# Expert 0's first layer with joint products for both parts of x, its results weighed by ScalarE, and the list work moved among the late tiles

## The chip, the cores and the metric

The kernel runs on one core of a Trainium2 chip. The metric is the device time of the whole program in microseconds (us). Engines are named as the profile names them: PE is TensorE's matmuls, PEld its weight loads, DVE is VectorE, ACT ScalarE, POOL GpSimd, SP SyncE, which issues DMAs. Each engine works through its own queue in the order in which the program was written.

## What is computed

Retention attention over 4 sequences of 768 tokens and 8 heads, whose rows are the tokens of a mixture of experts with one expert for each token:

```python
state = gamma * state + einsum(k_t, v_t);  y_t = scale * (q_t @ state)    # 3072 rows of 512
logits = x @ w_gate;  expert = argmax(logits);  gate_w = softmax(logits)[expert]
for e in range(8):
    h = maximum(x[mask] @ w1[e], 0)          # 512 -> 1024
    out[mask] = gate_w[mask] * (h @ w2[e])   # 1024 -> 512
```

Every float32 product of the experts is made of three: a number is cut into a high and a low part (`whi`, `wlo`; `xh`, `xl`; `hh`, `hl`), and TensorE adds up `whi*xh + wlo*xh + whi*xl` in one PSUM tile.

## The kernel before

The program runs in one pass that is written out by hand: what stands earlier in the code stands earlier in the queue of its engine, and nothing else sets the order.

**Retention** (`retention_moe`, up to 95 us of the profile) goes through 24 chunks of 128 tokens in 12 pairs k = 0 to 11. As tokens are finished, their expert is chosen in groups (`gating`), and GpSimd scatters their rows into a list of each expert in DRAM (`send_x`).

**Expert 0 is worked in two halves**, so that TensorE has work while the last lists are made. The **early half** (`early_half`) takes the first 192 tokens (EARLY) of expert 0. `hidden(f, part)` makes one of the 8 feature tiles of 128 with 12 matmuls of 192 columns (L823), each behind a weight load of its own; ScalarE then takes Relu into `rx` (L827) and a cast into `hh` (L828), and `low` subtracts to make `hl` (L831), for four tiles on VectorE and for four on GpSimd. `fill(n)` puts halves of tiles between the steps of the last gating. `result` is the second layer of 128 tokens, 24 matmuls of 512 columns (L841), weighed on VectorE (L845). The **late half** is e = 0 of `moe_main`: 224 tokens (LATE), 64 (BESIDE) of which share a row tile with the early rest. Its first layer is 8 tiles of 12 matmuls of 224 columns (L1052) into three PSUM tiles `phs` in turn; Relu and low part are made in two pieces of 64 and 160 columns (L1064, L1066). Its second layer has two row tiles of 24 matmuls (L1105), weighed on VectorE (L960), and a third one if the list is long.

**Lists.** Which experts come in which order (`eid`), where their lists end (`end`), how many tokens each has (`limit`) and by how much of its widest shape it stays short (`spare`) is worked out by some 16 small VectorE operations (L669 to L728) in the early half. TensorE's queue reads two of these numbers with loads of its own (`count_columns`, L896 and L897), called in late tile 4, and then branches over the four widths of expert 1's matmuls (`by_count`).

**Late x.** The late list is read from DRAM into `xg1`; VectorE transposes it in two pieces (L782), ScalarE casts one piece (L791) and VectorE the other (L718) to the high part, VectorE subtracts for the low part (L792, L720).

**Weights** come in parts of 1024 rows' worth, each cut by `split`: a ScalarE cast to `whi` (L172) and a VectorE subtraction to `wlo` (L174). Numbers 8 to 15 of expert 0's splits are halves of its second layer; of expert 1's parts, 0 is cut in late tiles 3 and 4, 1 in late tile 7, 2 beside the late second layer. `prep_x` transposes and cuts expert 1's x behind late tile 7. `jobs[f]` holds what is written behind late tile f (0 to 7) or behind step f - 8 of the second layer.

## Time and profile before

| | us |
|---|---|
| time, median of 3 runs | 386.64 (385.94 to 388.25) |
| the profiled execution, whole | 384.25 |
| its span in the profile | 382.40 |
| PE busy | 376.3 (98%) |
| DVE busy | 260.2 (68%) |
| the last 64 matmuls of the early first layer | 101.11 to 108.25 |
| early second layer | 108.25 to 113.77 |
| late first layer | 113.77 to 124.55 |
| late second layer | 124.55 to 135.66 |
| expert 1's first layer begins | 135.66 |

Times within the profile are from the start of its span. A row of the timeline gives start, length, engine, line, operation, output <- inputs, shape, and after an x how many instructions stand in it. Successive rows of PE overlap: the spacing of two starts, not a row's length, tells what a matmul costs TensorE.

### The profile page before, as it was taken

How to read it: one execution, taken by the hardware profiler on the slowest of the kernel's cores; microseconds unless marked ns; L12 is line 12 of the kernel's file. 1: busy time of each engine (PE TensorE's matmuls, PEld its weight loads, DVE VectorE, ACT ScalarE, POOL GpSimd, SP SyncE). 2: the span in 40 equal slices, each digit the busy share in tenths (PEclk: the TensorE clock that was granted, in tenths of full speed). 3: DMA queues.
4: the chain of work that ended last, by engine and by line, in shares of the span. 5: the costliest groups of instructions: out<-in, count | busy, mean ns of one | idle time of the engine just before them, and what ended most of it. 6: DMA issues, size and time to landing. Idle time of an engine off the chain costs nothing. (4 is left out here: it accounts for less than half of the span.)

```text
span 382.4 us, 8977 instructions
## 1 busy us (share of the span) xinstructions
PE 376.3 (98%) x3276; PEld 354.0 (93%) x3276; DVE 260.2 (68%) x571; ACT 154.8 (40%) x315; POOL 167.7 (44%) x149
## 2 busy tenths in 40 slices
PE   8999999999999999999999999999999999999994
PEld 5888888888989899999999999999999999999984
DVE  4548868798898786666675667486757767776511
ACT  3345445454734454334433542353434335444200
POOL 0332445647721230003853484357528444652754
PEclk9999999999999999999999999999999999999999
DMA  8998999997359765545664656366656756761111
GB/s 287 417 405 345 327 407 358 413 373 267 144 128 220 238 213 156 194 162 150 170 197 137 175 166 219 100 188 181 192 159 170 221 176 177 192 196 59 51 49 59
DMA packets 35237, 80.67 MB, mean 211 GB/s; under 512 B 5487, under 2 KB 19443, under 8 KB 33112
## 3 DMA queue, kind: packets, MB, share of 16 engines
q1 hardware_dynamic: 29892, 66.87, 54.0%
q0 software_dynamic: 5264, 12.69, 9.1%
q8 instruction: 58, 0.95, 1.1%
q14 instruction: 19, 0.16, 0.1%
q10 hardware_dynamic: 4, 0.01, 0.0%
HBM read 65.07 MB, written 15.19 MB: 210 GB/s over the span
## 5 line engine op out<-in xcount | busy, mean ns | idle before, releaser
L772 POOL DMA_INDIRECT out<-Z,sidx x82 | 104.8, 1278 | 120.5 <-DVE Z L991 102.9
L174 DVE TENSOR_TENSOR wlo<-raw,whi 128x1024 fp32r<-128x1024 f32 (+1 forms) x72 | 78.6, 1100 | 5.3 <-ACT whi L172 4.5
L1064 ACT ACTIVATE hh<-ph 128x64 fp32r<-128x64 f32 (+7 forms) x72 | 32.4, 461 | 91.5 <-PE ph L1052 91.5
L172 ACT CAST whi<-raw 128x1024 fp32r<-128x1024 f32 (+1 forms) x72 | 67.0, 952 | 5.2 <-DMA raw<-w 3.3
L1107 PE MATMUL py<-hh,wlo 128*128 128x392 f32 (+4 forms) x192 | 66.1, 344 | 0.0
L1107 PE MATMUL py<-hl,whi 128*128 128x392 f32 (+4 forms) x192 | 66.0, 344 | 0.0
L1107 PE MATMUL py<-hh,whi 128*128 128x392 f32 (+4 forms) x192 | 66.0, 344 | 0.0
L1066 DVE SCALAR_TENSOR_TENSOR hl<-ph,hh 128x64 fp32r<-128x64 f32 (+7 forms) x72 | 36.4, 515 | 34.1 <-ACT hh L1064 33.6
L1052 PE MATMUL ph<-xh,wlo 128*128 128x392 f32 (+5 forms) x224 | 49.1, 341 | 0.0
L1052 PE MATMUL ph<-xh,whi 128*128 128x392 f32 (+5 forms) x224 | 49.0, 341 | 0.0
L1052 PE MATMUL ph<-xl,whi 128*128 128x392 f32 (+5 forms) x224 | 48.9, 340 | 0.0
L1052 PEld LDWEIGHTS ph<-xh,whi 128*128 128x128 f32 x224 | 40.3, 189 | 0.3
L1052 PEld LDWEIGHTS ph<-xh,wlo 128*128 128x128 f32 x224 | 40.3, 188 | 0.2
L1052 PEld LDWEIGHTS ph<-xl,whi 128*128 128x128 f32 x224 | 40.3, 188 | 0.2
L281 POOL TENSOR_TENSOR vs<-qkv_t,cs 128x512 f32<-128x512 f32 x19 | 20.2, 1063 | 42.7 <-DMA qkv_t<-qkv 32.8
L1107 PEld LDWEIGHTS py<-hh,wlo 128*128 128x128 f32 x192 | 36.1, 188 | 0.2
L1107 PEld LDWEIGHTS py<-hh,whi 128*128 128x128 f32 x192 | 36.1, 188 | 0.2
L1107 PEld LDWEIGHTS py<-hl,whi 128*128 128x128 f32 x192 | 36.1, 188 | 0.2
L791 ACT CAST xh<-xt 128x512 fp32r<-128x512 f32 (+7 forms) x27 | 14.8, 551 | 50.7 <-DVE xt L782 50.7
L295 DVE TENSOR_TENSOR Sb<-sp,xgs 128x512 f32<-128x512 f32 x48 | 30.0, 683 | 4.8 <-PE sp L292 4.7
L772 POOL DMA_INDIRECT xs_dram<-xn,KEY x24 | 25.2, 1050 | 13.3 <-ACT xn L350 4.1
L986 DVE STREAM_TRANSPOSE Z<-py 128x416 f32<-128x416 f32 (+2 forms) x24 | 15.3, 637 | 20.4 <-PE py L1107 20.2
(168 smaller groups left out, 520.6 us busy)
## 6 DMA issues: line engine op xcount, KB each, us to landing
raw<-w SPq DMA_DIRECT2D x64, 512.0 KB
qkv_t<-qkv SPq DMA_DIRECT2D x16, 1024.0 KB
qkv_t<-qkv SPq DMA_DIRECT2D x8, 512.0 KB
qkv_t<-qkv SPq DMA_DIRECT2D x4, 768.0 KB
xgs<-xs_dram SPq DMA_DIRECT2D x12, 211.2 KB
xgs<-xs_dram SPq DMA_DIRECT2D x8, 227.5 KB
out<-Z,sidx POOLq DMA_INDIRECT x82, 3.8
xs_dram<-zero SPq DMA_DIRECT2D x6, 195.0 KB
```

Source lines behind the costliest of these rows:

```text
L172: nc.scalar.copy(out=to[h][:, a:a + n], in_=raw[:, a:a + n])
L174: engine.tensor_tensor(out=to[h][:, a:a + n], in0=raw[:, a:a + n], in1=parts[0][h][:, a:a + n].bitcast(F32), op=ALU.subtract)
L281: engine.tensor_tensor(out=vs, in0=qs[g][:, 2].rearrange("a (h d) -> a h d", d=D), in1=cv[:, c, :].unsqueeze(2).broadcast_to([P, H, D]), o ...
L295: nc.vector.tensor_tensor(out=Sb[:, r], in0=sps[r], in1=M[:, r], op=ALU.mult)
L772: sc = tc.nc.gpsimd.indirect_dma_start(out=out, out_offset=bass.IndirectOffsetOnAxis(ap=index, axis=0), in_=rows, in_offset=None, bounds_c ...
L791: nc.scalar.copy(out=xh[:, :, sl], in_=src)
L986: nc.vector.transpose(out=Zs[e][:, 0:nb, k, :], in_=py[:, 0:32 * nb].rearrange("p (j c) -> p j c", c=32))
L1052: nc.tensor.matmul(out=ph[:, :w], lhsT=sliver(wparts[e, f // 4][a], kd)[:, fo:fo + P], rhs=x[:, kd, :w], start=(n == 0), stop=(n == 3 * KD ...
L1064: nc.scalar.activation(out=to, in_=of, func=AF.Relu)
L1066: nc.vector.scalar_tensor_tensor(out=low, in0=of, scalar=0.0, in1=to.bitcast(F32), op0=ALU.max, op1=ALU.subtract)
L1107: nc.tensor.matmul(out=py[:, :cols], lhsT=sliver(a, f % 4)[:, k * P:(k + 1) * P], rhs=x[:, :cols], **se)
```

## The change

- **Joint products, early.** Tiles 1 to 7 of the early first layer have 4 matmuls `wlo*xh` of 192 columns and 4 matmuls of 384 columns, whose moving side is `xh` and `xl` side by side, with `whi` loaded once; tile 0 stays. The two halves of the PSUM tile are then added: ScalarE copies the second half into `rx`, VectorE adds the first (`join`), ScalarE takes Relu into `hh`, VectorE makes `hl` with max and subtract. All eight lows are on VectorE.
- **Joint products, late.** Tiles 1 to 7 of the late first layer likewise: 4 matmuls of 224 and 4 of 448 columns, a ScalarE copy and a VectorE addition into `sums` (the named `Z`); Relu and low part read `sums`.
- **Results of expert 0** are weighed by ScalarE.
- **Lists.** The 16 small operations leave the early half: they are `chores` of late tiles 0 to 5 (`before`, `numbers`, `ends`, `limits`, `spares`, `places`); `token_index` of the late rows goes from tile 2 to tile 6, the two loads of TensorE's queue from tile 4 to tile 7, part 0 of expert 1's splits behind late tile 7, part 1 into the second layer, part 2 to the second layer's second row tile.
- **Late x** is transposed in two pairs of its four slices, and ScalarE casts both.
- **Sooner.** The last rows are sent before, not behind, the early half's first VectorE work; SP reads the late list before it waits for expert 1's list end; the early list is read before the last parts of expert 0's weights; expert 0's second-layer splits begin one earlier (8 at k = 8).
- **Rank.** The last `rank` has a PSUM tile of another pool; FILL counts matmuls.

```diff
-FILL = (2, 2, 2, 2)
+FILL = (12, 8, 16, 16)
...
-SPLITS = {4: (0, 1), 5: (2, 3), 7: (4, 5), 8: (6, 7), 9: (8, 9), 10: (10,)}
+SPLITS = {4: (0, 1), 5: (2, 3), 7: (4, 5), 8: (6, 7, 8), 9: (9, 10), 10: (11,)}
...
+        products = [(f, i) for f, to in ((0, 8), (1, 4), (0, 12), (1, 8), *((f, 8) for f in range(2, KF)))
+                    for i in range({(0, 12): 8, (1, 8): 4}.get((f, to), 0), to)]
...
+            for f, i in products[state["done"]:state["done"] + n]:
+                hidden(f, i)
+            state["done"] += n
+
+        def joins(n):
+            for f in range(state["joined"], n):
+                join(f)
+            state["joined"] = n
...
             stages[name]()
-        split(0, 2, 3, nc.vector, 1, ("cast",))
         logits(NCH // 2 - 1)
         rows(NCH - 2)
+        finish_logits(NCH // 2 - 1)
         rows(NCH - 1)
-        finish_logits(NCH // 2 - 1)
         for g in range(SENDS[NCH // 2 - 1][1], GROUPS[-1][0]):
             send_x(g)
+        turned_rows = gsm.tile([P, 2], F32, name="turned_rows")
+        at = GROUPS[-1][0] % (2 * CPB)
+        nc.gpsimd.tensor_copy(out=turned_rows, in_=ring[:, at:at + 2, 0, 0])
...
         fill(FILL[1])
-        final["rank"](ps_s, "sp")
+        final["rank"](ps_m, "mm")
         fill(FILL[2])
         final["slots"]()
         final["weights"]()
-        split(0, 2, 3, nc.vector, 1, ("cut",))
-        past = gsm.tile([P, E1], F32, name="past")
+        for g in range(GROUPS[-1][0], NCH):
+            send_x(g)
+        joins(3)
...
         nc.vector.tensor_copy(out=end1, in_=past[:, 0:1])
+        joins(4)
         lows(2, nc.vector)
-        for g in range(GROUPS[-1][0], NCH):
-            send_x(g)
         for i in (12, 13):
-            split(0, *divmod(i, 4), nc.vector, 1)
+            split(0, *divmod(i, 4), nc.vector, 1, ("cast",))
         fill(FILL[3])
-        lows(4, nc.gpsimd)
-        sq = lambda name: gsm.tile([P, E1, E1], F32, name=name)
-        i7 = lambda t: t.unsqueeze(2).broadcast_to([P, E1, E1])
...
+        split(0, 3, 0, nc.vector, 1, ("cut",))
+        joins(5)
+        lows(3, nc.vector)
+        split(0, 3, 1, nc.vector, 1, ("cut",))
+        joins(6)
+        lows(4, nc.vector)
         for i in (14, 15):
-            split(0, *divmod(i, 4), nc.vector, 1)
-
-        nc.vector.tensor_tensor(out=se, in0=sel, in1=s7(past), op=ALU.mult)
-        with nc.allow_low_precision(reason="one nonzero term, an integer below 2**15"):
-            nc.vector.tensor_reduce(out=end7, in_=se, axis=AX.X, op=ALU.add)
+            split(0, *divmod(i, 4), nc.vector, 1, ("cast",))
+        fill(len(products) - state["done"])
...
+        split(0, 3, 2, nc.vector, 1, ("cut",))
+        joins(7)
+        lows(5, nc.vector)
+        split(0, 3, 3, nc.vector, 1, ("cut",))
+        lows(6, nc.vector)
+        joins(KF)
+        lows(KF, nc.vector)
         xg1 = ld.tile([P, NJ8, W], F32, name="xg1", tag="ld")
         xt1 = ld.tile([P, KD, LATE], F32, name="xt1", tag="ld")
         number = lambda i: nc.sync.value_load(eid7[0:1, i - 1:i], min_val=1, max_val=E - 1)
         end_of = lambda t, i: nc.sync.value_load(t[0:1, i - 1:i], min_val=0, max_val=(E9 + 1) * N)
-        past1 = end_of(end1, 1)
         load_x(xg1, E, NJ8)
         load_meta(meta0[EARLY - P:, 1:2], E, 1, 0, BESIDE)
         load_meta(meta0[:, 2:3], E, 1, BESIDE)
         load_meta(meta0[0:32, 3:4], E, 1, BESIDE + P, 32)
         fetch(1, 0)
+        past1 = end_of(end1, 1)
...
+        token_index(sidx0[:, 0:1], meta0[:, 0:1], cnt[:, 0:1])
...
+        xhl1 = new_xhl(LATE)
+        pairs = [slice(k, k + 2) for k in (0, 2)]
+        for ks in pairs:
+            turn_slices(nc, xt1, xg1, 0, LATE, None, ks)
+            nc.scalar.copy(out=xhl1[:, 0, ks], in_=xt1[:, ks])
+        for ks in pairs:
+            nc.vector.tensor_tensor(out=xhl1[:, 1, ks], in0=xt1[:, ks], in1=xhl1[:, 0, ks].bitcast(F32), op=ALU.subtract)
+        result(0, 0)
+        result(0, 1)
+        send(0)
...
+    chores = [before, numbers, ends, limits, spares, places]
...
-    def hidden(f, part):
-        whi, wlo = wparts[0, f // 4]
+    def hidden(f, i):
         fo = (f % 4) * P
-        if part != 1:
-            phs[f] = first if f == 0 else ps.tile([P, EARLY], F32, name="ph0", tag="sp")
-        order = [(a, x, kd) for a, x in ((whi, 0), (wlo, 0), (whi, 1)) for kd in range(KD)]
-        for i, (a, x, kd) in list(enumerate(order))[6 * part:6 * part + 6]:
-            nc.tensor.matmul(out=phs[f], lhsT=sliver(a, kd)[:, fo:fo + P], rhs=xhl[:, x, kd, :],
-                             start=(i == 0), stop=(i == len(order) - 1))
-        if part != 0:
+        whi, wlo = [[sliver(a, kd)[:, fo:fo + P] for kd in range(KD)] for a in wparts[0, f // 4]]
+        if i == 0:
+            phs[f] = first[f] if f < len(first) and first[f] is not None else ps.tile([P, 2 * EARLY], F32, name="ph0", tag="sp")
...
+        if f == 0:
+            todo = alone(whi, 0) + alone(wlo, 0) + alone(whi, 1)
+        else:
+            both = phs[f].rearrange("p (x t) -> p x t", x=2)
+            todo = alone(wlo, 0) + [(both, whi[kd], xhl[:, :, kd, :]) for kd in range(KD)]
+        to, w, x = todo[i]
+        nc.tensor.matmul(out=to, lhsT=w, rhs=x, start=(i == 0), stop=(i == len(todo) - 1), skip_group_check=True)
+        if i == len(todo) - 1:
             h = rx[:, f % 4, :]
-            nc.scalar.activation(out=h, in_=phs[f], func=AF.Relu)
-            nc.scalar.copy(out=hh[f][:, 0:EARLY], in_=h)
+            if f == 0:
+                nc.scalar.activation(out=h, in_=phs[f], func=AF.Relu)
+                nc.scalar.copy(out=hh[f][:, 0:EARLY], in_=h)
+            else:
+                nc.scalar.copy(out=h, in_=phs[f][:, EARLY:2 * EARLY])
+
+    def join(f):
+        h = rx[:, f % 4, :]
+        nc.vector.tensor_tensor(out=h, in0=phs[f][:, 0:EARLY], in1=h, op=ALU.add)
+        nc.scalar.activation(out=hh[f][:, 0:EARLY], in_=h, func=AF.Relu)
 
     def low(f, engine):
-        engine.tensor_tensor(out=hl[f][:, 0:EARLY], in0=rx[:, f % 4, :], in1=hh[f][:, 0:EARLY].bitcast(F32),
-                             op=ALU.subtract)
+        engine.scalar_tensor_tensor(out=hl[f][:, 0:EARLY], in0=rx[:, f % 4, :], scalar=0.0, in1=hh[f][:, 0:EARLY].bitcast(F32),
+                                    op0=ALU.max, op1=ALU.subtract)
...
-        nc.vector.tensor_scalar(out=sliced(yo[:w, j, :]), in0=featured(py[:w]), scalar1=meta0[:w, j, 1:2], scalar2=None,
-                                op0=ALU.mult)
+        nc.scalar.activation(out=sliced(yo[:w, j, :]), in_=featured(py[:w]), func=AF.Copy, scale=meta0[:w, j, 1:2])
...
+        if e == 0:
+            nc.scalar.activation(out=to, in_=turned, func=AF.Copy, scale=share)
+        else:
+            nc.vector.tensor_scalar(out=to, in0=turned, scalar1=share, scalar2=None, op0=ALU.mult)
...
-                job(2, nc.vector.memset, rare[0:widths[0][2]], 0.0)
-                job(2, token_index, sidx0[:, 1:4], meta0[:, 1:4], lim[:, 1:4], "joint")
+                for f, chore in enumerate(chores):
+                    job(f, chore)
+                job(KF - 2, token_index, sidx0[:, 1:4], meta0[:, 1:4], lim[:, 1:4], "joint")
+                job(KF - 1, nc.vector.memset, rare[0:widths[0][2]], 0.0)
                 for i in range(3):
-                    job(1 + i // 2, nc.vector.memset, phs[i][:, CAPS[1] - 3 * STEPS[1]:], 0.0)
+                    job(KF, nc.vector.memset, phs[i][:, 2 * LATE:], 0.0)
                 for j in range(nxt - 1):
                     job(KF - 1, prep_x, 1, j, nc.vector if j % 2 else nc.gpsimd)
...
+                job(4 if e else KF - 1, count_columns, e + 1)
             if e > 0:
...
-                for part, s0 in ((0, 3), (1, KF - 1)):
+                for part, s0, at in ((0, 3, KF - 1), (1, KF - 1, KF)):
                     job(s0, fetch, e + 1, part + 2)
                     for i, eng in halves:
-                        job(s0 + i * (s0 < KF - 1), split, e + 1, part, i, eng)
+                        job(at, split, e + 1, part, i, eng)
...
+                def beside_layer():
...
+                    main = ph[:, 0:LATE]
+                    both = ph[:, 0:2 * LATE].rearrange("p (x t) -> p x t", x=2)
+                    if f == 0:
+                        todo = [(main, a[kd], xh[:, kd]) for kd in range(KD) for a in (whi, wlo)]
+                        todo += [(main, whi[kd], xl[:, kd]) for kd in range(KD)]
+                    else:
+                        todo = [(main, wlo[kd], xh[:, kd]) for kd in range(KD)]
+                        todo += [(both, whi[kd], xhl1[:, :, kd]) for kd in range(KD)]
+                    for i, (to, w, x) in enumerate(todo):
+                        nc.tensor.matmul(out=to, lhsT=w, rhs=x, start=(i == 0), stop=(i == len(todo) - 1),
...
+                if e:
+                    by_count(e, first_layer)
+                else:
+                    beside_layer()
+                    if f == 0:
+                        sums = yp.tile([P, CMAX32 // 32, KD, 32], F32, name="Z").rearrange("p j k r -> p (j k r)")
+                    else:
+                        total = sums[:, f * LATE:(f + 1) * LATE]
+                        nc.scalar.copy(out=total, in_=ph[:, LATE:2 * LATE])
+                        nc.vector.tensor_tensor(out=total, in0=ph[:, 0:LATE], in1=total, op=ALU.add)
...
-                if more and e == 0 and k < 2:
-                    split(e + 1, 2, *halves[k])
+                if more and e == 0 and k == 1:
+                    for h in halves:
+                        split(e + 1, 2, *h)
```

What follows is VectorE's queue, in the program's order, at three places. `hl`, `hh`, `rx`, `xhl` are the parts named above; numbers behind a name tell one buffer from another; `Z` is `sums`; x2 stands for two alike.

**VectorE, from the last weight cuts of expert 0 (L174) to the late list's transposes, before:**

```order
L174 TENSOR_TENSOR wlo<-raw,whi 128x512 x2
L682 TENSOR_TENSOR se<-sel,past 128x49
L684 TENSOR_REDUCE end_84<-se 128x7
L831 TENSOR_TENSOR hl_1669<-rx_1664,hh_1667 128x192 x2
L704 TENSOR_SCALAR third<-cnt 128x1
L705 TENSOR_TENSOR se<-sel,cnt 128x49
L706 TENSOR_REDUCE limit<-se 128x7
L707 TENSOR_TENSOR limit<-limit,cs 128x7
L709 TENSOR_TENSOR fits<-limit,cs 128x21
L712 TENSOR_REDUCE spare<-fits 128x7
L782 STREAM_TRANSPOSE xt_1877<-xg_1876 128x4x4x32
L782 STREAM_TRANSPOSE xt_1877<-xg_1876 128x3x4x32
```

**The same place, after** (L872 is the addition of `join`, L876 the low part):

```order
L872 TENSOR_TENSOR rx_1666<-ph_1877,rx_1666 128x192
L876 SCALAR_TENSOR_TENSOR hl_1671<-rx_1666,hh_1669 128x192
L174 TENSOR_TENSOR wlo<-raw,whi 128x512
L876 SCALAR_TENSOR_TENSOR hl_1671<-rx_1666,hh_1669 128x192
L872 TENSOR_TENSOR rx_1666<-ph_1887,rx_1666 128x192
L876 SCALAR_TENSOR_TENSOR hl_1671<-rx_1666,hh_1669 128x192 x2
L230 TENSOR_SCALAR far<-cs,cnt 128x1
L232 TENSOR_SCALAR ids<-meta_81 128x1
L234 SCALAR_TENSOR_TENSOR sidx_82<-ids,far 128x1
L707 COPY lim<-cnt 64x1
L708 COPY lim<-cnt 64x1
L815 STREAM_TRANSPOSE xt_1909<-xg_1908 128x7x2x32 x2
```

The small list operations between the cuts and the transposes are gone; seven additions and four more low parts stand in the early half, each of which waits for a ScalarE operation, and the row numbers of the early tokens (L230 to L709) now stand ahead of the transposes.

**VectorE, between late tiles 2 and 5, before:**

```order
L1066 SCALAR_TENSOR_TENSOR hl_1668<-ph_2167,hh_1666 128x64
L1066 SCALAR_TENSOR_TENSOR hl<-ph_2167,hh 128x160
L1072 MEMSET between 32x512
L227 TENSOR_TENSOR far<-cs,lim 128x3
L228 TENSOR_SCALAR far<-far 128x3
L232 TENSOR_SCALAR ids<-meta_81 128x3
L1066 SCALAR_TENSOR_TENSOR hl_1668<-ph_2165,hh_1666 128x64
L1066 SCALAR_TENSOR_TENSOR hl<-ph_2165,hh 128x160
L174 TENSOR_TENSOR wlo<-raw,whi 128x1024
L1066 SCALAR_TENSOR_TENSOR hl_1669<-ph_2166,hh_1667 128x64
```

**Late tiles 3 to 5, after** (L1129 is the addition, L1139 the low part):

```order
L743 TENSOR_REDUCE end_84<-se 128x7
L1129 TENSOR_TENSOR Z<-ph_2020,Z 128x224
L1139 SCALAR_TENSOR_TENSOR hl_1670<-Z,hh_1668 128x64
L1139 SCALAR_TENSOR_TENSOR hl<-Z,hh 128x160
L749 TENSOR_SCALAR third<-cnt 128x1
L750 TENSOR_TENSOR se<-sel,cnt 128x49
L751 TENSOR_REDUCE limit<-se 128x7
L752 TENSOR_TENSOR limit<-limit,cs 128x7
L1129 TENSOR_TENSOR Z<-ph_2021,Z 128x224
L755 TENSOR_TENSOR fits<-limit,cs 128x21
L758 TENSOR_REDUCE spare<-fits 128x7
```

Each late tile has gained an addition and, up to tile 5, a list step, where one weight cut stood before.

**VectorE, from the last late tile to expert 1's weights, before:**

```order
L1066 SCALAR_TENSOR_TENSOR hl_1669<-ph_2167,hh_1667 128x64
L1066 SCALAR_TENSOR_TENSOR hl<-ph_2167,hh 128x160
L1066 SCALAR_TENSOR_TENSOR hl_1669<-ph_2166,hh_1667 128x64
L1066 SCALAR_TENSOR_TENSOR hl<-ph_2166,hh 128x160
L782 STREAM_TRANSPOSE xt<-xgs 128x4x4x32 x2
L792 TENSOR_TENSOR xl<-xt,xh 128x4x128
L782 STREAM_TRANSPOSE xt<-xgs 128x4x4x32
L782 STREAM_TRANSPOSE xt<-xgs 128x2x4x32
L792 TENSOR_TENSOR xl<-xt,xh 128x4x56
L174 TENSOR_TENSOR wlo<-raw,whi 128x1024 x2
```

**The same place, after:**

```order
L1129 TENSOR_TENSOR Z<-ph_2021,Z 128x224
L1139 SCALAR_TENSOR_TENSOR hl_1671<-Z,hh_1669 128x64
L1139 SCALAR_TENSOR_TENSOR hl<-Z,hh 128x160
L1145 MEMSET between 32x512
L815 STREAM_TRANSPOSE xt<-xgs 128x4x4x32 x2
L825 TENSOR_TENSOR xl<-xt,xh 128x4x128
L815 STREAM_TRANSPOSE xt<-xgs 128x4x4x32
L815 STREAM_TRANSPOSE xt<-xgs 128x2x4x32
L825 TENSOR_TENSOR xl<-xt,xh 128x4x56
L174 TENSOR_TENSOR wlo<-raw,whi 128x1024 x2
```

Expert 1's x (transposes L782, now L815) stands at the same place; before, two cuts of expert 1's first part (L174) stood some tiles ahead of it, and now both stand behind it.

## Rows read from the trace of the kernel before

**Rows 1.** Page, busy time of each engine and its share.
```profile
PE 376.3 (98%) x3276; PEld 354.0 (93%) x3276; DVE 260.2 (68%) x571; ACT 154.8 (40%) x315; POOL 167.7 (44%) x149
```

**Rows 2.** Waits of PEld from 95 to 136 us: total, times, longest.
```profile
PEld ph L823 <- ACT xn L350: 0.2, 1, 0.2
```

**Rows 3.** Windows: four stages of expert 0, busy time of each engine.
```profile
100.00:108.20 8.20, 8.17 (x77) 8.15 (x76) 7.66 (x23) 6.67 (x19) 6.19 (x8) 1.00 0.36 134
108.20:113.70 5.50, 5.50 (x26) 4.52 (x26) 5.01 (x18) 1.31 (x3) 0.00 (x0) 1.00 0.65 131
113.70:124.50 10.80, 10.80 (x97) 10.80 (x97) 8.99 (x35) 4.78 (x16) 1.00 (x1) 1.00 0.92 220
124.50:135.60 11.10, 11.10 (x51) 8.99 (x51) 8.53 (x12) 5.79 (x10) 3.04 (x3) 1.00 0.80 259
```

**Rows 4.** Timeline of PE, expert 0's four stages.
```profile
101.11 1.06 PE L823 MATMUL ph<-xhl,whi 128*128 128x192 f32 x8
...
108.25 0.41 PE L841 MATMUL py<-whi,hh 128*128 128x512 f32 x1
...
113.77 0.60 PE L1052 MATMUL ph<-xhl,whi 128*128 128x224 f32 x4
...
114.65 1.09 PE L1052 MATMUL ph<-xhl,whi 128*128 128x224 f32 x8
...
124.55 0.41 PE L1105 MATMUL py<-whi,hh 128*128 128x512 f32 x1
```

**Rows 5.** Timeline of PE: tiles 1 and 2 of expert 1's first layer.
```profile
137.84 0.86 PE L1052 MATMUL ph<-xh,whi 128*128 128x392 f32 x4
...
139.97 0.87 PE L1052 MATMUL ph<-xh,whi 128*128 128x392 f32 x4
```

**Rows 6.** DVE groups by shape: busy, mean ns | idle before.
```profile
L295 DVE TENSOR_TENSOR Sb<-sp,xgs 128x512 f32<-128x512 f32 x48 | 30.0, 683 | 4.8 <-PE sp L292 4.7
...
L1066 DVE SCALAR_TENSOR_TENSOR hl<-ph,hh 128x160 fp32r<-128x160 f32 x8 | 2.5, 306 | 0.0
...
L1066 DVE SCALAR_TENSOR_TENSOR hl<-ph,hh 128x64 fp32r<-128x64 f32 x8 | 1.8, 224 | 1.9 <-ACT hh L1064 1.9
...
L831 DVE TENSOR_TENSOR hl<-rx,hh 128x192 fp32r<-128x192 f32 x4 | 1.2, 350 | 0.0
```

**Rows 7.** ACT groups by shape: busy, mean ns | idle before.
```profile
L172 ACT CAST whi<-raw 128x512 fp32r<-128x512 f32 x16 | 9.3, 631 | 0.0
...
L827 ACT ACTIVATE rx<-ph 128x192 f32<-128x192 f32 x8 | 2.6, 326 | 1.5 <-PE ph L823 1.3
```

**Rows 8.** Timeline of DVE from 101 to 132 us.
```profile
101.36 0.68 DVE L174 TENSOR_TENSOR wlo<-raw,whi 128x512 fp32r<-128x512 f32 x1
...
102.90 0.62 DVE L831 TENSOR_TENSOR hl<-rx,hh 128x192 fp32r<-128x192 f32 x2
103.44 1.28 DVE L174 TENSOR_TENSOR wlo<-raw,whi 128x512 fp32r<-128x512 f32 x2
104.64 2.65 DVE L669 SCALAR_TENSOR_TENSOR c<-cnt,cs 128x7 f32<-128x7 f32 x1
...
110.81 0.20 DVE L706 TENSOR_REDUCE limit<-se 128x7 f32<-128x49 f32 x1
...
111.80 1.17 DVE L782 STREAM_TRANSPOSE xt<-xg 128x512 f32<-128x512 f32 x2
...
125.57 1.29 DVE L782 STREAM_TRANSPOSE xt<-xgs 128x512 f32<-128x512 f32 x2
...
131.68 2.53 DVE L174 TENSOR_TENSOR wlo<-raw,whi 128x1024 fp32r<-128x1024 f32 x2
```

**Rows 9.** Line views: loads of TensorE's queue in `count_columns`, ns and place.
```profile
L896 PEldq TENSOR_LOAD <-third x1: 752/752/752, 118.5 to 118.5; - x1
...
L897 PEldq TENSOR_LOAD <-spare x7: 306/316/322, 119.7 to 320.0; - x7
L897 PEldq SEQ_ASSERT  x7: 18/18/18, 120.3 to 320.6; - x7
```

More of the change, by code (lines that the diff above doesn't have):

```diff
@@ L257, in retention_moe @@
         qs, vss, Sbs, xTs, lgs, Ys = {}, {}, {}, {}, {}, {}
-        state = {"half": 0, "low": 0}
+        state = {"done": 0, "low": 0, "joined": 1}
         half = (slice(0, D), slice(D, P))
@@ L558, in retention_moe @@
                 stages["advance"]()
-                if not last:
+                if k < 10:
                     stages["weights"]()
@@ L697, in retention_moe, with before, numbers, ends @@
         fetch(1, 1)
+        token_index(sidx0[:, 0:1], meta0[:, 0:1], cnt[:, 0:1])
+        nc.vector.tensor_copy(out=lim[0:EARLY - P, 1:2], in_=cnt[0:EARLY - P, 0:1])
+        nc.vector.tensor_copy(out=lim[EARLY - P:, 1:2], in_=cnt[EARLY - P:, E:E9])
+        nc.vector.tensor_copy(out=lim[:, 2:4], in_=cnt[:, E:E9].broadcast_to([P, 2]))
+        xhl1 = new_xhl(LATE)
[8 more added lines that the diff above has]
+        send(0)
+    sq = lambda name: gate.tile([P, E1, E1], F32, name=name)
+    i7 = lambda t: t.unsqueeze(2).broadcast_to([P, E1, E1])
+    c8, pos = [gate.tile([P, E1], F32, name=n) for n in ("c8", "pos")]
+    gt = sq("gt")
+    fits = gate.tile([P, 3, E1], F32, name="fits")
+    far = gate.tile([P, E1, JMAX], F32, name="far")
+    def before():
+        nc.vector.scalar_tensor_tensor(out=c8, in0=cnt[:, 1:E], scalar=float(E), in1=k_("rev"),
+                                       op0=ALU.mult, op1=ALU.add)
+        nc.vector.tensor_tensor(out=gt, in0=s7(c8), in1=i7(c8), op=ALU.is_gt)
+        nc.vector.tensor_reduce(out=pos, in_=gt, axis=AX.X, op=ALU.add)
+    def numbers():
+        nc.vector.tensor_tensor(out=sel, in0=s7(pos), in1=i7(iota[:, 0:E1]), op=ALU.is_equal)
+        nc.vector.tensor_tensor(out=se, in0=sel, in1=s7(k_("eid")), op=ALU.mult)
+        with nc.allow_low_precision(reason="one nonzero term, a small integer"):
+            nc.vector.tensor_reduce(out=eid7, in_=se, axis=AX.X, op=ALU.add)
+    def ends():
+        nc.vector.tensor_tensor(out=se, in0=sel, in1=s7(past), op=ALU.mult)
+        with nc.allow_low_precision(reason="one nonzero term, an integer below 2**15"):
+            nc.vector.tensor_reduce(out=end7, in_=se, axis=AX.X, op=ALU.add)
         for i in range(2, E):
@@ L750, in retention_moe @@
     natural = {0: (sidx0, meta0)}
[L751 removed]
+    moe_main(tc, chores, wparts, fetch, split, leave, one_more, xhl1, hidden_early, third, lim, xgs, clear_behind, load_x, load_meta, token_index, regions, beyond, limit, spare, natural,
              overflow, out)
@@ L850, in send, with moe_main @@
         scatter_rows(tc, out, sidx0[:w, j:j + 1], yo[:w, j, :])
-    return hidden, low, result, send, (hh, hl)
+    return hidden, join, low, result, send, (hh, hl)
 @with_exitstack
-def moe_main(ctx, tc, wparts, fetch, split, leave, one_more, xhl1, hidden_early, third, lim, xgs, clear_behind, load_x, load_meta, token_index, regions, beyond, limit, spare, natural,
+def moe_main(ctx, tc, chores, wparts, fetch, split, leave, one_more, xhl1, hidden_early, third, lim, xgs, clear_behind, load_x, load_meta, token_index, regions, beyond, limit, spare, natural,
              overflow, out):
```

65 lines of the change are left out of this document (18 added, 47 removed).

## Prediction

> **What bounds the kernel now.** I read the busy times first: PE is busy 98% of the span [rows 1]. Then the waits of the weight loads in the stretch that the change touches: one, of 0.2 us, before the last rank [rows 2]. Through expert 0's four stages TensorE works without a gap, at a granted clock of 1.00, 35.57 of 35.60 us [rows 3]. So a microsecond of matmul taken away shortens the kernel by one, as long as nothing else becomes late; and what could become late is read from the other engines in the same rows. VectorE is the next: 7.66 of 8.20, 5.01 of 5.50, 8.99 of 10.80 and 8.53 of 11.10 us. It has little to give, above all in the first two stages. That is the tension of this case: the change saves TensorE time and pays for it with VectorE work.
>
> The profiled execution took 384.25 us, 2.4 below the median of 386.64. Every term below is a difference on its clock and is carried over to the median.
>
> **What a joint product saves.** Spacings come from the starts of PE [rows 4, 5]. Early tiles: 101.11 to 108.25 is 64 matmuls of 192 columns, 0.1116 each. Late tiles: 114.65 to 124.55 is 88 matmuls of 224 columns, 0.1125 each. Nearly the same for more columns: here something other than columns sets the spacing, and the weight loads, busy as long as PE in these two stages [rows 3], are the candidate. 512 columns: 108.25 to 113.77 is 24, 0.230 each. 392 columns: 137.84 to 139.97 is 12, 0.1775 each. Between the last two a column costs 0.00044, so 384 columns are worth 0.174 and 448 columns 0.202.
>
> An early tile costs 12 x 0.1116 = 1.34 now and 4 x 0.1116 + 4 x 0.174 = 1.14 then: 0.20 less, for seven tiles **1.37**. A late tile costs 1.35 now and 4 x 0.1125 + 4 x 0.202 = 1.26 then: 0.09 less, for seven tiles **0.61**. Together **1.98 us**.
>
> **What an addition costs VectorE.** No row shows one of 192 or 224 columns from PSUM and SBUF. Below: the low part of 160 columns, 306 ns; above: the addition of 512 columns with the same two sources, 683 ns [rows 6]. The two low parts (64 columns 224 ns, 160 columns 306 ns) give 0.85 ns for a column, so 333 and 361 ns; the subtraction of 192 columns from SBUF took 350. And the 512-column addition took no longer (683) than the 512-column cut from SBUF (0.68) [rows 6, 8], so PSUM adds nothing. I take 0.35 to 0.36, of which the next instruction sees 0.28: two subtractions of 0.35 took 0.62 together [rows 8]. The ScalarE copies are bounded likewise by Relu of 192 columns, 326 ns [rows 7].
>
> **Early half: TensorE comes sooner, late x does not.** With 1.37 saved TensorE is free for late x at 112.40, where before it began at 113.77. On VectorE the end of the list work (L669, 2.65 us beside GpSimd's low parts, and some 15 of about 0.2 behind it) goes [rows 8]. What stands there then, from 101.1 on: 7 additions x 0.28, 8 low parts x 0.27, 4 cuts x 0.60 (two took 1.28), 5 small steps of `past` and 6 for the early rows' numbers at 0.15 to 0.2 each, 8.3 us in all. By that alone it would reach late x at 109.4. But it works in order, and each tile goes from ScalarE (copy) to VectorE (add) to ScalarE (Relu) to VectorE (low part), while four casts of 0.63 stand between on ScalarE [rows 7]. Writing both queues down in their new order with these durations, VectorE waits 0.3 for the second addition, 0.5 for the first cast, 0.7 for the third cast, which stands behind the Relu of tile 5, and 0.7 in small pieces: 2.2 us. It comes to the transposes at 111.6 (before: 111.80 [rows 8]). The first pair takes 0.6, its ScalarE cast 0.6, with 0.13 for the hand-overs: the late half starts at 112.93, **0.53 late**.
>
> The lists land sooner, since the sends and SP's late list move ahead; that costs nothing, and gives nothing while VectorE itself arrives at 111.6. Were they to land after that, each 0.1 would cost 0.1. Weighing results on ScalarE takes 0.75 three times off VectorE and is covered by a ScalarE that is busy 4.78 of 10.80 there [rows 3]. The splits moved into k = 8 and the pool of the last rank's tile I cost at nothing: retention's ScalarE and VectorE have gaps there; if not, TensorE stands for part of one split, 0.6. The wait of 0.2 before the last rank [rows 2] remains, and takes some 0.05 of the first joint tile's saving.
>
> **Late first layer: the shapes of expert 1 are known late.** Call its start S. Each joint tile costs VectorE 1.1 (addition 0.28, low parts 0.41, and 0.4 of waiting for ScalarE's Relu between them), and the list steps of tiles 1 to 6 add 3.2: 0.2 for each of 16 small operations, like L706 [rows 8]. TensorE passes a tile in 1.26. The first addition comes at S + 3.2, so the step that makes `spare`, behind tile 4, ends at S + 3.2 + 4 x 1.1 + 2.2 = S + 9.8. Only then can TensorE's queue load it; that load took from 119.7 to 120.3 [rows 9], 0.64. It stands behind late tile 7's matmuls, so the second layer waits for it: it starts at S + 10.6 at the soonest, where the matmuls end at S + 1.35 + 7 x 1.26 = S + 10.2. **0.4 late.** The three PSUM tiles suffice: tile 4's addition ends at S + 8.7, tile 7 wants its tile at S + 8.9.
>
> **Expert 1's first weights.** The last low part is done at S + 14.2, with one memset S + 14.7. Expert 1's x took from 125.57 to 131.68, 6.1, and the two cuts behind it 2.5 [rows 8]. Before, part 0 had been cut in late tiles 3 to 5; now it is cut behind x, and ends at S + 23.2. The second layer takes 11.1 (124.55 to 135.66), expert 1 starts at S + 21.7, and six matmuls of 0.1775 later, at S + 22.7, it needs the second half of `wlo`: **0.5 late**. Four more cuts (parts 1 and 2) stand ahead of its first low part, which costs its fourth tile about **0.15**.
>
> **The sum.** -1.98 + 0.05 + 0.53 + 0.4 + 0.5 + 0.15 = -0.35 us: 383.9 for the profiled execution, **386.3** for the median. I forecast a change too small to be measured: most of TensorE's saving is eaten by VectorE.
>
> **What a rule says.** Where 192 and 224 columns cost the same here [rows 4], the Trainium skill (TensorE: Matmul & The Clock Gate, Back-to-back issue gap) gives N/2.4 + 2.5 ns for a matmul alone, which for 192 and 384 columns is 82.5 and 162.5 ns: by it a joint tile would save an estimated 0.01 us, and the whole change 0.15. The page itself says that the formula leaves out the weight load and is too small for few columns; the 0.1116 of this trace agrees with that remark and not with the formula.
>
> **The rivals.**
> *The cover holds* (0.17): VectorE's waits for ScalarE fall into gaps, spare is there before TensorE's queue asks, and the cuts are in time. Then -1.98 + 0.05 and perhaps 0.1 of remains: 384.7. For it: each of the four waits is only 0.15 to 0.5 long, and an addition at the lowest bound (0.306) takes 0.05 off fourteen of them, 0.6 in all. Against it: VectorE had 0.5 free in each of the first two stages.
> *VectorE becomes the bound* (0.14, ends slower): all fourteen additions lie on its chain, so each 0.1 by which they exceed 0.35 costs 14 x 0.1 = 1.4. It decides from 0.38 on; at 0.45 the time is 387.7, at 0.51 it is 388.5, and at the upper bound of 0.683 it would be 390.9. For it: PSUM is read by ScalarE and written by TensorE meanwhile. Against it: the 512-column pair shows no price of PSUM.
> *Joint products save nothing* (0.06): if a column's cost under a shared weight load is that of the 512-column row throughout, a tile costs 8 x 0.1116 - 4 x 0.230 = 0.03 more; fourteen of them +0.4. VectorE's waits then mostly vanish, since TensorE comes no sooner: 387.0. Against it: 392 columns took 0.1775.
>
> **How the numbers follow.** The forecast has 0.63. A difference of 0.5% (1.93 us, below 384.7 or above 388.6) is about what a measurement of this kernel can tell from no change. Faster: most of the first rival and a little of the forecast, 0.18. Slower: the part of the second rival in which additions cost over 0.51, and misplaced cover, 0.10. Same: 0.72. The range of 384.4 to 388.5 reaches from the full cover to additions of 0.51.
>
> **What would show it.** In the profile of after: starts of joint matmuls 0.174 and 0.20 apart (if 0.23, the third rival); additions of 0.35 (if over 0.45, the second); first transposes of late x near 111.6 and a wait of PE there for ScalarE's cast; a PE gap before the second layer of the late half behind the load of `spare`; a wait for `wlo` in expert 1's first tile. If these three gaps are missing, the first rival holds. The prediction is wrong altogether if TensorE waits somewhere in retention, or if the late list lands after 112.

## The result: 0.8% slower

| | before | after |
|---|---|---|
| time, median of 20 runs each | 385.72 us | 388.50 us |
| ratio after/before, 95% interval | | 1.0079 (1.0050 to 1.0108) |
| the profiled execution's span | 382.40 | 386.30 |
| PE busy | 376.3 | 375.8 |
| its first matmul of the early half, from the span's start | 95.23 | 95.32 |
| behind that: early second layer begins | 13.02 | 12.72 |
| late first layer begins | 18.53 | 20.00 |
| late second layer begins | 29.32 | 30.78 |
| expert 1's first layer begins | 40.42 | 43.84 |
| expert 1's second layer begins | 57.50 | 61.04 |
| the end of the span | 287.15 | 290.94 |

The forecast was 386.3 with a chance of 0.10 for slower. In the table the first loss lies between the early second layer and the late first layer (0.30 ahead becomes 1.47 behind), the second in front of expert 1 (1.46 becomes 3.42). Behind expert 1 the difference grows by only 0.25 more.

After, the waits of PE itself from 95 to 175 us (engine, what waited, released by: total, times, longest). Before, PE had none in this stretch; the 0.2 of [rows 2] is a weight load's:

```profile
PE ph L1101 <- DVE ph L1209: 1.7, 1, 1.7
PE ph L1116 <- ACT xhl L714: 1.1, 1, 1.1
PE Y L861 <- ACT rx L868: 0.4, 1, 0.4
PE L L364 <- DVE rk L424: 0.3, 1, 0.3
PE py L1178 <- PE ph L1116: 0.2, 1, 0.2
```

Of these five the prediction had three: the late start (L1116), the second layer behind the load of `spare` (L1178) and one at expert 1 (L1101), but there with another cause. The timeline of PE after (the rows that answer to [rows 4]; start, length, engine, line, what, shape, how many; in brackets the idle time and its releaser):

```profile
100.40 0.67 PE L861 MATMUL Y<-xhl,wlo 128*128 128x192 f32 x4
100.91 0.88 PE L861 MATMUL Y<-xhl,whi 128*128 128x384 f32 x4
102.20 0.69 PE L861 MATMUL Y<-xhl,wlo 128*128 128x192 f32 x4 [0.41 <-ACT rx L868]
102.73 0.88 PE L861 MATMUL Y<-xhl,whi 128*128 128x384 f32 x4
103.45 0.59 PE L861 MATMUL ph<-xhl,wlo 128*128 128x192 f32 x4
...
104.59 0.59 PE L861 MATMUL ph<-xhl,wlo 128*128 128x192 f32 x4
...
115.31 0.37 PE L1116 MATMUL ph<-xhl,whi 128*128 128x224 f32 x1 [1.14 <-ACT xhl L714]
...
117.27 0.99 PE L1116 MATMUL ph<-xhl,whi 128*128 128x448 f32 x4
118.10 0.60 PE L1116 MATMUL ph<-xhl,wlo 128*128 128x224 f32 x4
118.53 0.99 PE L1116 MATMUL ph<-xhl,whi 128*128 128x448 f32 x4
...
139.16 0.95 PE L1101 MATMUL ph<-xh,whi 128*128 128x392 f32 x4 [1.70 <-DVE ph L1209]
```

The joint products do what they should: an undisturbed early tile takes 1.14 (103.45 to 104.59, forecast 1.14), a late one 1.26 (117.27 to 118.53, forecast 1.26). What is new stands at 102.20. Early tiles 2 and 3 are both in `Y`, one PSUM tile, in halves that share no column; yet tile 3 starts only when ScalarE has copied tile 2 (101.83 + 0.32). ScalarE and VectorE at the same place:

```profile
101.83 0.32 ACT L868 COPY rx<-Y 128x192 f32<-128x192 f32 x1 [0.39 <-PE Y L861]
103.65 0.32 ACT L868 COPY rx<-Y 128x192 f32<-128x192 f32 x1 [1.50 <-PE Y L861]
```

```profile
101.47 0.36 DVE L872 TENSOR_TENSOR rx<-ph,rx 128x192 f32<-128x192 f32 x1
104.00 0.36 DVE L872 TENSOR_TENSOR rx<-Y,rx 128x192 f32<-128x192 f32 x1 [2.17 <-ACT rx L868]
...
113.97 1.17 DVE L815 STREAM_TRANSPOSE xt<-xg 128x448 f32<-128x448 f32 x2
...
136.58 3.57 DVE L174 TENSOR_TENSOR wlo<-raw,whi 128x1024 fp32r<-128x1024 f32 x3
138.94 0.07 DVE L1209 MEMSET ph<- 128x4 f32 x3
```

VectorE's addition of tile 2 (104.00) has its input since 102.15, when ScalarE's copy of tile 2 ended. It starts when the copy of tile 3 is done, at 103.97; TensorE had reported tile 3 done by a semaphore, a counter on which other engines wait, at 103.63 already. All of VectorE's queue stands behind this addition. The last two rows are the second place: three memsets of four columns of `ph`, columns that expert 1's first matmuls do not write, stand behind two cuts of expert 1's weights (the third cut of that row comes after them), and PE waits for them (139.16).

### The profile page after: what moved, and what is told of

Same layout as the page of the kernel before. It is cut to its first block, busy times and chain, and to the rows that moved or that the text cites. A ratio compares the mean times of both kernels' runs of the same rounds, so it can differ in the third digit from the quotient of the medians.

```text
span 386.3 us, 8881 instructions
## 1 busy us (share of the span) xinstructions
PE 375.8 (97%) x3220; PEld 350.5 (91%) x3220; DVE 260.1 (67%) x584; ACT 159.4 (41%) x327; POOL 165.5 (43%) x146
## 5 line engine op out<-in xcount | busy, mean ns | idle before, releaser
L174 DVE TENSOR_TENSOR wlo<-raw,whi 128x1024 fp32r<-128x1024 f32 (+1 forms) x72 | 78.4, 1099 | 5.4 <-ACT whi L172 4.8
L1137 ACT ACTIVATE hh<-ph 128x440 fp32r<-128x440 f32 (+8 forms) x58 | 29.4, 508 | 82.5 <-PE ph L1101 81.7
L1139 DVE SCALAR_TENSOR_TENSOR hl<-ph,hh 128x440 fp32r<-128x440 f32 (+8 forms) x58 | 33.3, 576 | 33.0 <-ACT hh L1137 32.7
L1101 PE MATMUL ph<-xh,whi 128*128 128x392 f32 (+5 forms) x224 | 49.2, 341 | 1.7 <-DVE ph L1209 1.7
L1101 PE MATMUL ph<-xh,wlo 128*128 128x392 f32 (+5 forms) x224 | 49.2, 341 | 0.0
L1101 PE MATMUL ph<-xl,whi 128*128 128x392 f32 (+5 forms) x224 | 49.0, 340 | 0.0
L1101 PEld LDWEIGHTS ph<-xh,whi 128*128 128x128 f32 x224 | 40.4, 188 | 2.2 <-ACT whi L172 2.0
L1101 PEld LDWEIGHTS ph<-xh,wlo 128*128 128x128 f32 x224 | 40.5, 188 | 0.2
L1101 PEld LDWEIGHTS ph<-xl,whi 128*128 128x128 f32 x224 | 40.4, 188 | 0.2
```

What stands on the lines that cost most here:

```text
L174: engine.tensor_tensor(out=to[h][:, a:a + n], in0=raw[:, a:a + n], in1=parts[0][h][:, a:a + n].bitcast(F32), op=ALU.subtract)
L1101: nc.tensor.matmul(out=ph[:, :w], lhsT=sliver(wparts[e, f // 4][a], kd)[:, fo:fo + P], rhs=x[:, kd, :w], start=(n == 0), stop=(n == 3 * KD ...
L1137: nc.scalar.activation(out=to, in_=of, func=AF.Relu)
L1139: nc.vector.scalar_tensor_tensor(out=low, in0=of, scalar=0.0, in1=to.bitcast(F32), op0=ALU.max, op1=ALU.subtract)
```

## The experiments

My theory after this comparison: the prediction's walk was right but lacked two releases, the shared tile `Y` (2.3 us on VectorE's queue) and the memsets (1.2 us at expert 1). The main rival: VectorE simply has too much work with fourteen additions. Ratios are to the kernel before, run beside on the same chip. The runs came in three batches, in which the kernel before took 384.7, 391.9 and 391.8 us, so times of different batches are not compared, only ratios. In the timelines I give times behind the first matmul of the early half, as in the table.

### Tile 3 out of the shared tile

```diff
-*(Y2[:, r].rearrange("a g t -> a (g t)")[:, 0:2 * EARLY] for r in range(2))],
+*(Y2[:, r].rearrange("a g t -> a (g t)")[:, 0:2 * EARLY] for r in range(1))],
```

> Only early tile 3 changes: it gets a PSUM tile of the rotating pool instead of the second half of the tile Y that tile 2 also stands in. Theory (shared tile): in the changed kernel tile 3 waits for ScalarE's copy of tile 2 (0.41 us) and VectorE's addition of tile 2 waits for ScalarE's copy of tile 3 (104.00 instead of 101.7), which moves VectorE's whole queue by 2.3. Then here the addition of tile 2 starts at about 101.8, the late half at 112.9 to 113.2 instead of 115.31, expert 1 at about 136.9 instead of 139.16, and the time is 2.2 to 2.4 below the changed kernel, 0.2% over the kernel before. Rival (VectorE has too much work with fourteen additions, whoever it waits for): the late half starts at 114.6 or later and the gain is under 0.7.

Measured: 1.0050 (1.0019 to 1.0081). The late half began at 17.47 instead of 20.00, expert 1 at 41.34 instead of 43.84, and the span from the first early matmul fell from 290.94 to 288.44. VectorE's additions in this trace:

```profile
101.86 0.35 DVE L872 TENSOR_TENSOR rx<-ph,rx 128x192 f32<-128x192 f32 x1
102.36 0.36 DVE L872 TENSOR_TENSOR rx<-Y,rx 128x192 f32<-128x192 f32 x1 [0.16 <-ACT rx L868]
103.51 0.36 DVE L872 TENSOR_TENSOR rx<-ph,rx 128x192 f32<-128x192 f32 x1
```

The addition of tile 2 follows that of tile 1 by 0.50, where it was 2.53. VectorE has as many additions as in the changed kernel, so its amount of work was not what delayed the late half. In the timed runs the gain was smaller than in the trace and than expected: 0.3% of the ratio, 1.1 us, against 2.5, and the interval overlaps that of the changed kernel (1.0050 to 1.0108). What shows the cause is the trace, not the time.

### The memsets ahead of expert 1's x

```diff
-                    job(KF, nc.vector.memset, phs[i][:, 2 * LATE:], 0.0)
+                    job(KF - 1, nc.vector.memset, phs[i][:, 2 * LATE:], 0.0)
```

> Only the three small memsets of ph move: behind late tile 7 ahead of expert 1's x, instead of behind the two cuts of expert 1's first weights. Theory (the memset is the last release of expert 1's first matmul): that matmul no longer waits for the cuts (1.70 us at 139.16), only its sixth to eighth matmul wait some 0.5 for the second cut; expert 1 ends 1.1 to 1.3 sooner and the time is about 1.2 below the changed kernel, 0.45% over the kernel before. Rival (the cuts themselves are the wait): the same 1.7 appears in the middle of the first tile and the gain is under 0.3.

Measured: 1.0063 (1.0035 to 1.0092), 0.6 us of the ratio where 1.2 was expected, and within the interval of the changed kernel. In the trace:

```profile
139.64 0.22 PE L1188 MATMUL between<-whi,hh 128*32 128x128 f32 x1
139.70 0.93 PE L1101 MATMUL ph<-xh,whi 128*128 128x392 f32 x4
140.46 0.52 PE L1101 MATMUL ph<-xh,wlo 128*128 128x392 f32 x2
141.42 0.62 PE L1101 MATMUL ph<-xh,wlo 128*128 128x392 f32 x2 [0.44 <-DVE wlo L174]
```

Expert 1 starts without a gap, and the wait that the prediction had forecast, for the second cut of `wlo`, appears where it was forecast, before the seventh matmul, with 0.44 of idle (forecast 0.5). From the late start to expert 1's second layer it took 40.08 instead of 41.04: 0.96 of the 1.70 came off.

### Both

> Both edits. Theory: the two losses are in different places and add up, 3.3 to 3.6 below the changed kernel, ratio to the kernel before 0.997 to 1.000; this is the kernel that the prediction had computed. Rival (VectorE's work is the bound): 1.003 or more.

Measured: 1.0026 (0.9994 to 1.0058), and on another chip the same kernel again:

> The kernel with both edits again, beside the next one on the same chip. Theory: ratio 1.000 to 1.003.

Measured: 1.0030 (0.9998 to 1.0061). Of the loss of 0.79% some 0.5% is gone, 1.9 to 2.0 us, against 3.3 to 3.6 expected. Both intervals reach 1, and by 0.1% also that of the changed kernel; both centres lie above the forecast. In the traces the two gains did not add up: the span from the first early matmul is 288.67 with both edits and was 288.44 with the first alone. The milestones of the first trace show how far the walk held, as differences to before:

| | forecast | changed kernel | both edits | both edits, again |
|---|---|---|---|---|
| early second layer | -1.37 | -0.30 | -1.31 | -1.30 |
| late first layer | -0.84 | +1.47 | -0.89 | +0.07 |
| late second layer | -1.0 | +1.46 | -0.89 | +0.08 |
| expert 1's first layer | -1.0 | +3.42 | -0.77 | +0.19 |
| expert 1's second layer | -0.4 | +3.54 | +1.14 | +1.76 |

The first trace of both edits is the forecast to 0.25 up to expert 1. Then it loses 1.9 in expert 1's first layer where 0.65 was forecast. About 0.9 of that is the wait for `wlo` (0.7) and the one in front of the fourth tile (0.2), from the spacings between matmuls. The rest, 0.94, is a gap before the second layer, which the profile puts down to ScalarE; in the second trace, the last row, it puts the same gap down to nothing that it shows ("issue"):

```profile
151.92 0.87 PE L1101 MATMUL ph<-xl,whi 128*128 128x392 f32 x4
153.57 0.44 PE L1180 MATMUL py<-hh,whi 128*128 128x392 f32 x1 [0.78 <-ACT hh L1137]
```

```profile
161.68 0.44 PE L1180 MATMUL py<-hh,whi 128*128 128x392 f32 x1 [0.39 <-issue]
```

The view of the branch line, over which TensorE's queue comes to that layer (operation, count, shortest, median and longest ns):

```profile
L953 PEldq COMPARE_BRANCH  x44: 207/208/3798, 131.1 to 357.3; - x44
```

One branch of 44 took 3.80 us; it is the one at 149.71, and it ended 0.06 before the second layer's first matmul. In the second trace of the same kernel it took 3.41 and also ended 0.06 before that matmul. In the kernel before no branch took over 2.16, and the two on the way to this layer took 0.42 and 0.21. That the gap is the branch's is read from these times; no run tests it.

In the second trace the late half began 1.0 later, although the matmuls of TensorE's early tiles started alike to 0.02. ScalarE's copy of tile 2 came later. The first rows are of the first trace, where the early half began at 94.93, the second of the other, where it began at 102.43:

```profile
101.11 0.32 ACT L868 COPY rx<-Y 128x192 f32<-128x192 f32 x1 [0.46 <-PE Y L861]
```

```profile
109.42 0.32 ACT L868 COPY rx<-Y 128x192 f32<-128x192 f32 x1 [1.27 <-PE Y L861]
```

6.18 against 6.99 behind the first early matmul. The last matmul of tile 2 started 5.80 behind it in both. ScalarE itself was not late: as the brackets say, its wait was ended by TensorE. The semaphore on which the copy waits was raised at 101.09 in the first trace and at 109.40 in the second, 0.02 before the copy in both, which is 0.36 and 1.17 behind the start of tile 2's last matmul. The next copy was 1.1 late in the same way; the signal of tile 5 was on time again, 9.6 behind the first early matmul in both. The granted clock was 1.00 through the early half of both. Why TensorE's signals came late is open. Of the nine traces in which tile 2 was made at that time, three have the copy at 6.18 to 6.32 and six at 6.96 to 7.00; both of the first batch are among the three, all four of the third among the six.

### The shared tile, by tiles 2 and 4

```diff
-*(Y2[:, r].rearrange("a g t -> a (g t)")[:, 0:2 * EARLY] for r in range(2))],
+*(t for r in range(2) for t in (Y2[:, r].rearrange("a g t -> a (g t)")[:, 0:2 * EARLY], None))],
```

> The memsets moved as before, and the tile Y is still shared by two early tiles, but by 2 and 4 instead of 2 and 3 (3 gets a tile of the rotating pool). Theory (it is the order in which the program names the shared tile that costs: tile 3 written between tile 2's copy and tile 2's addition): with tile 4 behind that addition nothing waits, so the late half starts as with a tile of its own, 17.5 to 17.9 us behind the first early matmul, and the time is within 0.1% of the kernel with both edits. Rival (two tiles in one PSUM tile cost by themselves): the late half starts 1 to 2.4 later.

Measured: 1.0026 (0.9999 to 1.0053), like both edits on that chip (1.0030). The late start was 19.32, not 17.5 to 17.9; on that chip it was 18.60 with a tile of its own, so 0.7 is left to the sharing (VectorE's addition of tile 2, TensorE's tile 4):

```profile
110.98 0.36 DVE L872 TENSOR_TENSOR rx<-Y,rx 128x192 f32<-128x192 f32 x1 [1.16 <-issue]
...
111.40 0.69 PE L861 MATMUL Y<-xhl,wlo 128*128 128x192 f32 x4 [0.48 <-DVE rx L872]
```

With the copies late in this trace (tile 2's at 7.00), the addition of tile 2 (110.98 to 111.34) was late, and tile 4 waited for it, again across columns it does not touch. So the order of the program is not all: here the shared tile cost something because the reader ahead was late. The theory's first half holds, that the two halves wait for each other as one; its second half, that two tiles' distance makes it free, fell.

### Which joint products pay

Early half without joint products (twelve single matmuls, Relu and cast on ScalarE, no additions), with both edits:

```diff
-FILL = (12, 8, 16, 16)
+FILL = (12, 12, 24, 24)
...
-        if f == 0:
+        if True:
             todo = alone(whi, 0) + alone(wlo, 0) + alone(whi, 1)
...
     def join(f):
...
+        pass
...
```

> As with both edits, and the early half's tiles 1 to 7 made of twelve single matmuls again, with Relu and cast on ScalarE and no addition; all eight low parts stay on VectorE. Theory: TensorE takes 1.37 longer in the early half, VectorE's queue is 2.0 of work and some of its waits shorter, so TensorE's end sets the late start, at 113.8 to 114.0; 0.6 to 1.0 slower than with joint products, ratio to the kernel before about 1.000 to 1.002. Rival (the joint form costs VectorE more than it gives TensorE): faster than with both edits.

Measured: 1.0046 (1.0027 to 1.0066): 0.8 us of the ratio slower than with them, as expected, though the intervals overlap and the ratio itself was expected at 1.000 to 1.002; the late start was 18.64, 1.0 later.

Late half without them, with both edits (the three memsets of `ph` then clear 60 columns each instead of four):

```diff
-                    job(KF, nc.vector.memset, phs[i][:, 2 * LATE:], 0.0)
+                    job(KF - 1, nc.vector.memset, phs[i][:, CAPS[1] - 3 * STEPS[1]:], 0.0)
...
-                    if f == 0:
+                    if True:
                         todo = [(main, a[kd], xh[:, kd]) for kd in range(KD) for a in (whi, wlo)]
...
-                        nc.scalar.copy(out=total, in_=ph[:, LATE:2 * LATE])
-                        nc.vector.tensor_tensor(out=total, in0=ph[:, 0:LATE], in1=total, op=ALU.add)
```

> As with both edits, and the late half's tiles made of twelve single matmuls again, Relu and low part straight from PSUM, no copy and no addition. Theory: TensorE takes 0.6 longer in the late first layer, but VectorE's backlog of 4 us at its end shrinks to 1, so that the waits for spare (0.24) and for expert 1's wlo (0.45 and 0.15) go: between 0.3 below and 0.2 above the kernel with both edits. Rival (the late joint products are worth what TensorE saves): 0.5 to 0.7 above it, ratio 1.004 or more.

Measured: 0.9989 (0.9964 to 1.0013), by ratio 1.4 us below both edits of the first batch, where at most 0.3 was expected. And again beside both edits:

> Both edits and the late half without joint products again. Theory: 0.3 to 1.3 below the kernel with both edits, since its first matmuls of expert 1's second layer come 56.9 behind the first early matmul against 57.9 with the joint form there. Rival: equal.

Measured: 1.0004 (0.9985 to 1.0022) against 1.0030, 1.0 us. Twice the same sign, though each pair of intervals overlaps: by the centres the late joint products cost more than they give. In the traces of the second pair the late first layer then takes 10.89 instead of 10.80, so a saving of 0.6 has shrunk to 0.1: with joint products 0.62 lies between the start of its last matmul and that of the second layer, of which a matmul takes 0.2, and the rest is the wait for `spare`. And expert 1's first layer takes 17.17 instead of 18.65 (18.99 in the first trace of both edits), without any wait of PE in it. VectorE shows where this comes from. Its cuts of expert 1's first weights, with late joint products (first row) and without (second row), in the same two traces:

```profile
142.38 4.69 DVE L174 TENSOR_TENSOR wlo<-raw,whi 128x1024 fp32r<-128x1024 f32 x4
```

```profile
140.09 4.70 DVE L174 TENSOR_TENSOR wlo<-raw,whi 128x1024 fp32r<-128x1024 f32 x4
```

They begin 39.95 and 37.45 behind the first early matmul, while TensorE begins expert 1 at 40.61 and 40.57. In the late half, then, the additions do make VectorE late, by 2.5 us.

Neither half with joint products, with both edits:

> As with both edits, and no joint product in either half: what is left of the change are the moved lists, sends, splits and the results weighed by ScalarE. Theory: TensorE is the bound throughout as in the kernel before, ratio 0.999 to 1.002. Rival (the moves have a price of their own, in expert 1's first layer): 1.004 or more.

Measured: 1.0001 (0.9978 to 1.0023). The moved lists, sends and weighings neither cost nor give anything that this measurement can tell. The kernel with late joint products alone (1.0046, 1.0027 to 1.0066) has an interval that parts from this one: 0.45% by the centres, though the two ratios are of different batches.

### Taking the forecast waits away

```diff
-    chores = [before, numbers, ends, limits, spares, places]
+    chores = [before, numbers, limits, spares, ends, places]
...
-                    for a, x in ((0, xh), (1, xh), (0, xl)):
+                    for a, x in ((0, xh), (0, xl), (1, xh)) if e == 1 else ((0, xh), (1, xh), (0, xl)):
```

and the early rows' numbers and limits (`token_index`, three copies to `lim`) behind the late x.

> As with both edits (1.0026 of the kernel before), and three small moves against the waits that its trace still shows: the early rows' numbers behind late x's transposes (late start waits 0.3 for ScalarE's cast), the limits and spares two tiles sooner, ahead of the ends (the second layer waits 0.24 for TensorE's load of spare), and expert 1's first layer takes xl ahead of wlo (0.45 wait for the second cut of wlo). Theory (these are the prediction's three terms and each is a wait that can be taken away): 0.8 to 1.1 below the kernel with both edits, ratio 0.999 to 1.001. Rival (VectorE's queue is full, so a wait taken away here comes back behind): under 0.3 below it.

Measured: 1.0004 (0.9978 to 1.0030). The ratio moved as expected. Of the three, the load's wait went (late first layer 10.49); expert 1's first layer took 18.33 instead of 18.99, for the wait for `wlo` shrank from 0.7 to 0.3, but 0.2 came in front of the second tile, and the wait in front of the fourth, for VectorE's low part, grew from 0.2 to 0.7; the late start did not come sooner than in the first trace of both edits (17.79 against 17.64), and in this trace too the copy of tile 2 was late, at 6.96.

The same three moves, and joint products in the early half alone:

> Joint products in the early half alone, with the three small moves: the cheap half of VectorE's load. Theory: the late start waits no more, nothing else waits, and the early saving of 1.37 stays whole: ratio 0.9965 to 0.9985, the fastest of all. Rival (a wait takes its place): 1.000 or more.

Measured: 0.9984 (0.9950 to 1.0017), the lowest of all and within the expected range, with an interval that reaches 1. PE still waited 0.4 at its late start, 17.85, which missed the expectation. And with both edits, joint products in the early half alone, and only the three copies to `lim` moved:

> As the one before it, and the three copies of the list limits stand behind late x's transposes on VectorE, 0.45 us of work. Theory (VectorE sets the late start): the late half starts 0.4 sooner, 17.3 behind the first early matmul, ratio 0.996 to 0.999. Rival (ScalarE's copies come later again, as when all six steps were moved): no gain.

Measured: 1.0020 (0.9995 to 1.0045); the late start was 18.32 against 18.56 beside it, 0.24 sooner where 0.4 was expected, and the time was not lower. I have no version that can be told from the kernel before; the best centres are 0.1 to 0.2% below it.

## Why the prediction was wrong

- **What bounds the kernel, what a joint product saves, what an addition costs**: right. Tiles took 1.14 and 1.26 as forecast; the additions 0.353 to 0.355 (192 columns) and 0.382 (224), forecast 0.35 and 0.36. Two slips in its sums change next to nothing: seven late tiles at 1.35 - 1.258 save 0.64, not 0.61, and the third rival's difference is 4 x 0.230 - 8 x 0.1116 = 0.03.
- **"Early half: TensorE comes sooner, late x does not"**: the step that failed. Both queues were written down in order with the right durations, and each operation was made to wait for its own inputs alone. That two feature tiles now live in one PSUM tile was not weighed, though the change puts them there in one line. The prediction's "0.3 for the second addition" is this wait, and it measured 2.17. It made the late start 2.3 later than forecast (+1.47 against -0.84), since the chain from ScalarE to VectorE and back, rightly named as the tension, begins with just this addition. With a tile of its own the wait was 0.16 and 0.34 in the first two traces, and in the second of them the late start came at -0.89. So close a match is partly luck: over the eight traces in which no early tile is shared and the early products are joint, two of them with the early numbers moved and one with the limits alone, it lies between -1.07 and +0.07.
- **The last rank's tile and the splits in retention, costed at nothing**: the trace of the changed kernel has a wait of 0.28 (97.25), but behind the last rank but one, whose tile the change leaves alone, and none of the traces with an edit shows it. Its cause is open.
- **The wait for `spare`, forecast 0.4**: 0.61 between the last two starts where a matmul takes 0.2. The right place and size; with `spare` made two tiles sooner it went.
- **Expert 1's first weights, forecast 0.5 and 0.15**: these waits were there (0.7 and 0.2 by spacings) once the memsets were out of their way. In the changed kernel the memsets took their place with 1.70. This is the second step that failed: the "one memset" of the prediction's count is that of `between` (0.48), and the three of `ph`, which the diff moves behind step 8, where two cuts stand ahead, are nowhere in it, nor is the question who waits for them.
- **The rivals**: VectorE's being the bound was put down to the price of an addition. That price was right, and the delay of the early half came from what VectorE waited for. In the late half this rival was nearer: at the forecast price the additions left VectorE 2.5 us behind at expert 1's weights. The joint products did save.
- Not settled: the two edits took 2.5 and 1.1 us off the traces one by one, 2.3 together, and 1.1, 0.6 and 1.9 to 2.0 off the timed runs, and the kernel with both is 0.3% slower than before where -0.1% was forecast. In its traces I see two causes that no row of before showed, the gap behind the long branch (0.5 to 0.9) and TensorE's late signals for ScalarE's copies (1.0 at the late start). What makes either was not tried.

## What to carry to other kernels

When a change puts two results into one buffer to save space, walk the queues with the buffer, not its columns, as what is waited for: each writer behind every earlier reader, each reader behind every earlier writer, and here even a reader behind the reader before it (the addition of tile 2 behind the copy of tile 3). For every small operation that a change moves, a memset above all, ask which engine's next step has its release as the last. And a saving on the bound engine that is paid on the second busiest is worth only the part for which that engine has time: here, by centres whose intervals mostly overlap, the early joint products, at 0.20 saved a tile, paid 0.1 to 0.2% of the time and the late ones, at 0.09, cost 0.3 to 0.5%.

## What the runs showed that I had not expected

- A branch of TensorE's queue, 0.21 us at the median of 44, took 3.80 and 3.41 us ahead of expert 1's second layer in two traces of one kernel. The longer of the two branches on the way to that layer took 1.4 to 2.2 in the changed kernel and in all other variants with the late joint products, 0.4 in the kernel before, in the one without joint products and in three of the four with joint products in the early half alone, and 2.1 in the fourth. Where it ended just before the matmul, PE stood still, and the profile named another engine in one trace and none in the other. Branches of 2.0 to 3.1 us also stand elsewhere in several of these traces, so they do not belong to the joint products alone.
- The semaphore that tells ScalarE of early tile 2 was raised 0.4 us behind the start of that tile's last matmul in some traces and 1.2 in others, of one kernel too, with the matmuls started alike. It is the first link of the chain that sets the late start: between the two traces of one kernel 0.81 there went with 0.96 at the late start.
